# A decode kernel's tail: w4 in four pieces instead of five, and the first sums merged in two ways

## The chip, the cores and the metric

The kernel runs on one core of a Trainium2 chip. The metric is the device time of one execution in microseconds (us); less is better. Beside it stands the span, from the first to the last instruction of the program in the profile of the same kernel, which leaves out about 2 us at the edges. Each execution that was timed has one of each.

Engines are named as in the profile: PE is TensorE's matmuls, PEld its weight loads, DVE is VectorE, ACT is ScalarE. `L226` is a line of the kernel.

## The reference, cut to what matters

One token passes through two branches whose results are added to x: attention over a long cache with four key/value heads, and a small MLP.

```python
xn = _layernorm(x, axis=-1)
return x + _A_ref(xn, A_k_cache, A_v_cache, A_wq, A_wo) + _B_ref(xn, B_w1, B_w2, B_w3, B_w4)
# _A_ref: ... softmax(q k^T) v ... @ wo       caches of 4 x 65536 x 128 each
# _B_ref: ... h2 = gelu(layernorm(x1) @ w3) @ w4;  return x1 + h2     w4 is 3584 x 1024
```

About 170 MB are read and 2 KB written. The last thing read is w4: 28 rows of 128x1024 numbers in the kernel's layout (a "row" below is one of these 28, 256 KB of bfloat16).

## The kernel before

The loads stand in one queue and come in order (the pieces of w4 landed at 384.1, 391.4, 394.6, 395.8 and 396.4 us in the trace before); w4 is the last, in pieces of 8, 12, 5, 2 and 1 rows, so that its rows can be used while the next pieces come.

```python
W4_PIECES = (8, 12, 5, 2, 1)
FIRST = 3
AT_ONCE = 1
NARROW = 8
AHEAD = 5
...
for n in W4_PIECES:
    go(out=t[:, c0 * D:(c0 + n) * D], in_=w4_v[:, c0:c0 + n, :].rearrange("p c n -> p (c n)"))
```

The first 20 rows are "wide": two matmuls of 512 columns each into `psB`. The last 8 rows are "narrow": four matmuls of 256 columns into two other banks, `quarters`, so that four 32-column tiles of the array work side by side (in the trace before the first four start within 0.01 us, at 394.59 us, and take 0.28 us each). Between the fifth and the sixth narrow row the sums of the wide rows and of the attention are put into `quarters` by two small fp32 matmuls ("injection").

```python
early = sum(W4_PIECES[:AT_ONCE])
compute_w4(0, FIRST)
with tc.issue_after(tail["gathered"]):
    compute_w4(FIRST, early)
projected = project(HKV - 1)                       # attention, last head, into psB
with tc.issue_after(projected):
    compute_w4(early, FC - NARROW)                 # wide rows
sums = ogpool.tile([64, 512], F32, name="sums", tag="og")
nc.vector.tensor_tensor(out=sums[:], in0=psB[0:64, :], in1=tail["o"], op=ALU.add)
...
narrow_rows(FC - NARROW, FC - NARROW + AHEAD, start=True)
...
for h in range(2):                                 # fp32, 64x64 tiles
    nc.tensor.matmul(quarters[h][64 * h:64 * h + 64, 0:256], lhsT=pick[:]..., rhs=sums[:, 256 * h:256 * (h + 1)],
                     start=False, stop=False, tile_position=(0, 64 * h), skip_group_check=True)
narrow_rows(FC - NARROW + AHEAD, FC)
out_t = ogpool.tile([64, 2, 256], BF16, name="out_t", tag="og")
nc.scalar.copy(out=out_t[:, 0, :], in_=quarters[0][0:64, 0:256])
nc.vector.tensor_copy(out=out_t[:, 1, :], in_=quarters[1][64:128, 0:256])
nc.scalar.dma_start(out=out[0, 0, :].rearrange("(j n) -> j n", j=2), in_=out_t[31:33].rearrange("p h n -> p (h n)"))
```

## Time and profile before

| | before |
|---|---|
| median time, 3 runs | 401.07 us (400.98 to 402.7) |
| span of the profiled execution | 398.6 us |
| last landing of w4 | 396.44 us |
| end of the last matmul | 396.77 us |

From the page of the kernel before: the span, the engines' busy time, and the load queue with packets, MB and its share of the 16 DMA engines' time.

```profile
span 398.6 us, 2575 instructions
...
PE 225.4 (57%) x1360; PEld 44.0 (11%) x866; DVE 210.7 (53%) x160; ACT 27.1 (7%) x35; POOL 5.8 (1%) x29
...
q1 hardware_dynamic: 4128, 169.87, 98.9%
```

No compute engine is near full; the load queue is. The kernel is bound by its stream, and a change to its tail can hardly do more than shift what happens between the end of the stream and the end of the program. The chain that ended last in the kernel before (start, duration, what; its last four steps) says the same:

```profile
363.32 33.11 DMA big<-in_B_w_dram
396.44 0.04 issue
396.48 0.34 PE pm_r L501 x4
396.84 0.43 DVE out_t L522
```

The last landing, at once four matmuls, the cast, the store. TensorE in this stretch of the kernel before (start, duration, line, what, count, and in brackets the idle time before it and what ended that):

```profile
388.28 1.90 PE L227 MATMUL psB<-big,oT 128*32 128x512 bf16 x16
391.49 2.77 PE L227 MATMUL psB<-big,hT 128*32 128x512 bf16 x24 [1.30 <-DMA big<-in_B_w_dram]
394.59 0.73 PE L501 MATMUL pm_r<-big,hT 128*32 128x256 bf16 x20 [0.34 <-DMA big<-in_B_w_dram]
395.25 0.65 PE L516 MATMUL pm_r<-sums,pick 64*64 64x256 f32 x4
395.83 0.40 PE L501 MATMUL pm_r<-big,hT 128*32 128x256 bf16 x8
396.48 0.29 PE L501 MATMUL pm_r<-big,hT 128*32 128x256 bf16 x4 [0.24 <-DMA big<-in_B_w_dram]
```

The last four matmuls waited 0.24 us for the last row, so everything before them was done in time. And TensorE stood idle for 1.30 us before the 12-row piece.

### The profile page before, as it was taken

To read this page: it belongs to the slowest core of one execution; us is meant where nothing else is said; L and a number is where in the kernel's file an instruction comes from. 1 tells how busy PE (TensorE), PEld (TensorE's weight loads), DVE (VectorE), ACT (ScalarE), POOL (GpSimd) and SP (SyncE) were. 2 spreads that over 40 slices of the span, in tenths; PEclk is the share of its full clock that TensorE was granted. 3 is DMA by queue.
4 is the path that set the end of the run, shared out by engine and by line. 5 is a ranking of instruction groups with operands and counts; after the bars stand their busy time and mean duration, and the time that the engine had idled before them with its cause. 6 is when DMAs were issued, how large, how long until landed. Compare 5 with 4: busy or idle time off the path is not lost.

```text
span 398.6 us, 2575 instructions
## 1 busy us (share of the span) xinstructions
PE 225.4 (57%) x1360; PEld 44.0 (11%) x866; DVE 210.7 (53%) x160; ACT 27.1 (7%) x35; POOL 5.8 (1%) x29
## 2 busy tenths in 40 slices
PE   0251960591569238733974296519462955394986
PEld 0210000010100010011001010200020101010132
DVE  0610010974296559633963795269439942894141
ACT  1001020003000200020002000200110001002000
POOL 2000000000000000000000000000000000000000
PEclk9995996596869787966695889679956896698799
DMA  9998999999999999999999999999999998999996
GB/s 421 421 443 376 446 427 480 454 421 421 416 428 427 421 467 449 427 421 427 423 441 421 447 454 434 416 427 421 441 436 427 447 447 383 416 462 424 413 432 257
DMA packets 4144, 170.03 MB, mean 427 GB/s; under 512 B 419, under 2 KB 421, under 8 KB 678
## 3 DMA queue, kind: packets, MB, share of 16 engines
q1 hardware_dynamic: 4128, 169.87, 98.9%
q8 instruction: 9, 0.15, 0.2%
q14 instruction: 1, 0.01, 0.0%
q10 hardware_dynamic: 6, 0.00, 0.0%
HBM read 169.87 MB, written 0.00 MB: 426 GB/s over the span
## 4 chain that ended last, share of the span: by engine, by line
DMA 56%; DVE 21%; PE 17%; ACT 2%; another core or an unknown queue 2%; issue 1%; SPq 0%; DVEq 0%; ACTq 0%
DMA big<-in_A_k_cache_dram 42%; DVE big L360 15%; PE sc L365 11%; DMA big<-in_B_w_dram 8%; DMA big<-in_A_wq_dram 6%; PE oacc L415 4%; DVE p_sb L386 2%; DVE mx L370 2%; ACT p_sb L383 2%; PE psq L290 1%; SPq L187 0%; PE pm_mx L372 0%; DVE m L374 0%; PE pm_mx L379 0%
## 5 line engine op out<-in xcount | busy, mean ns | idle before, releaser
L365 PE MATMUL sc<-big,qdiag 128*128 128x512 bf16 x512 | 129.6, 414 | 66.5 <-DVE big L360 61.0
L360 DVE STREAM_TRANSPOSE big<-big 128x4096 f32<-128x4096 f32 x32 | 139.4, 4413 | 50.1 <-DMA big<-in_A_k_cache_dram 50.1
L415 PE MATMUL oacc<-big,p_sb 128*32 128x512 bf16 x512 | 43.2, 504 | 34.5 <-DVE p_sb L386 34.5
L370 DVE TENSOR_REDUCE mx<-sc 128x1 f32<-128x2048 f32 x8 | 18.3, 2292 | 29.9 <-PE sc L365 29.9
L365 PEld LDWEIGHTS <-qdiag 128*128 128x128 bf16 x128 | 13.2, 103 | 178.3 <-issue 145.7
L383 ACT ACTIVATE p_sb<-sc,nball 128x2048 bf16<-128x2048 f32 x8 | 15.7, 1968 | 220.8 <-DVE nball L381 220.8
L386 DVE STREAM_TRANSPOSE p_sb<-p_sb 128x2048 bf16<-128x2048 bf16 x8 | 18.5, 2311 | 18.0 <-ACT p_sb L383 18.0
L415 PEld LDWEIGHTS <-p_sb 128*32 128x32 bf16 x512 | 16.2, 122 | 58.2 <-DVE p_sb L386 35.1
L290 PE MATMUL psh<-big,ln_rep_b 128*32 128x512 bf16 (+1 forms) x64 | 12.4, 942 | 8.9 <-DMA big<-in_B_w_dram 8.9
L455 PE MATMUL o_acc<-big,oT 128*1 128x512 bf16 x48 | 13.2, 447 | 2.4 <-ACT p_sb L383 2.4
L372 PE MATMUL pm_mx<-ident_f,mx 128*1 128x128 f32 x8 | 2.4, 296 | 19.1 <-DVE mx L370 19.1
L424 DVE SCALAR_TENSOR_TENSOR og<-oacc,wb,og 128x512 f32<-128x512 f32 x4 | 3.0, 751 | 18.5 <-PE oacc L415 18.5
L329 DVE STREAM_TRANSPOSE h_row<-h_row 128x896 bf16<-128x896 bf16 x1 | 1.1, 1111 | 22.0 <-ACT h_row L328 22.0
L241 PE MATMUL pm_ln<-ln_rowsum_a,ones_f 128*128 128x1 f32 x2 | 0.6, 348 | 12.8 <-DVE ln_rowsum_a L239 12.8
L437 PE MATMUL pm_e<-ol,sel8big 128*128 128x129 f32 x8 | 2.3, 370 | 9.7 <-DVE ol L436 9.7
L314 POOL COPY qdiag<-qx 32x32 bf16<-32x32 bf16 x16 | 3.3, 204 | 278.7 <-PE sc L365 250.7
L290 PE MATMUL psq<-big,ln_rep_a 128*32 128x512 bf16 x64 | 5.0, 479 | 3.7 <-DMA big<-in_A_wq_dram 3.7
L232 DVE STREAM_TRANSPOSE x_t<-x_row 32x256 bf16<-32x256 bf16 x4 | 2.5, 615 | 8.4 <-DMA x_row<-in_A_x_dram 8.3
L466 DVE TENSOR_TENSOR big<-o_acc,big 1x512 f32<-1x512 f32 x2 | 1.4, 679 | 10.3 <-PE o_acc L455 10.3
L227 PE MATMUL psB<-big,hT 128*32 128x512 bf16 x40 | 4.8, 380 | 1.4 <-DMA big<-in_B_w_dram 1.3
L302 DVE CAST q_row<-psq 128x512 bf16<-128x512 f32 x1 | 0.7, 692 | 7.6 <-PE psq L290 7.6
L379 PE MATMUL pm_mx<-ident_f,rep 1*128 1x1 f32 x8 | 1.8, 229 | 5.0 <-DVE rep L376 5.0
(100 smaller groups left out, 71.9 us busy)
## 6 DMA issues: line engine op xcount, KB each, us to landing
big<-in_A_wo_dram SPq DMA_DIRECT2D x1, 8192.0 KB, 35.7
big<-in_B_w_dram SPq DMA_DIRECT2D x1, 7168.0 KB, 38.1
big<-in_B_w_dram SPq DMA_DIRECT2D x3, 2048.0 KB, 35.5
big<-in_B_w_dram SPq DMA_DIRECT2D x1, 3072.0 KB, 29.5
big<-in_B_w_dram SPq DMA_DIRECT2D x1, 1280.0 KB, 32.2
big<-in_B_w_dram SPq DMA_DIRECT2D x1, 512.0 KB
big<-in_B_w_dram SPq DMA_DIRECT2D x1, 256.0 KB, 33.1
big<-in_A_k_cache_dram SPq DMA_DIRECT2D x8, 42.2
```

The lines of the kernel that those rows point to most:

```text
L227: return nc.tensor.matmul(psB[32 * j:32 * j + 32, :], lhsT=lhsT.to_broadcast([lhsT.shape[0], 32]), rhs=rhs, start=start, stop=False, tile_ ...
L232: nc.vector.transpose(out=x_t[32 * a:32 * a + 32].rearrange("p c j -> p (c j)"), in_=x_row[:, 256 * a:256 * (a + 1)].rearrange("p (i c) -> ...
L290: nc.tensor.matmul(acc[32 * q:32 * q + 32, i, 0:n], lhsT=rep[:, c, :], rhs=cols(c, i, q), start=(c == 0), stop=(c == DC - 1), tile_positio ...
L314: nc.gpsimd.tensor_copy(out=qdiag[at, LEAD:].rearrange("p (x c) -> p x c", x=4)[:, :, 32 * a:32 * a + 8], in_=qx[at, :, 8 * g:8 * g + 8])
L360: nc.vector.transpose(out=words, in_=words)
L365: nc.tensor.matmul(sc[:, e, :], lhsT=qdiag[:, c0:c0 + P], rhs=cols[:, s, e, :, b2, :, r], start=(s == 0 and b2 == 0 and r == 0), stop=(s = ...
L370: nc.vector.reduce_max(out=mx[:], in_=sc[:].rearrange("p e n -> p (e n)"), axis=AX.X)
L383: nc.scalar.activation(out=p_sb[:], in_=sc[:], func=ACTF.Exp, bias=nball[:, b:b + 1], scale=SCALE, accum_out=group["lall"][:, b:b + 1])
L386: nc.vector.transpose(out=flat, in_=flat)
L415: mm = nc.tensor.matmul(oacc[32 * q:32 * (q + 1), :], lhsT=pT[:, e, 32 * t:32 * (t + 1)], rhs=vt[:, :, e, t, :], start=(e == 0 and t < 4), ...
L424: nc.vector.scalar_tensor_tensor(out=og[:], in0=oacc[:], scalar=wb[:, 1:2], in1=og[:], op0=ALU.mult, op1=ALU.add)
L455: nc.tensor.matmul(tail["rows"][0:1, h2, :], lhsT=oT[g][:, j:j + 1], rhs=wt[:, g, j, 512 * h2:512 * (h2 + 1)], start=(g == 0 and j == 0), ...
```

## The change

The intent: one load less in the tail (9, 13, 5, 1 rows), and the sums brought over more cheaply. The attention's part is injected early, in TensorE's idle time. The wide rows' sums are copied out as two halves, one by ScalarE and one by VectorE; the first is injected between the narrow rows, the second is added by VectorE in the cast that it does anyway. So one injection is left between the narrow rows where there were two.

```diff
-W4_PIECES = (8, 12, 5, 2, 1)
-FIRST = 3
-AT_ONCE = 1
-NARROW = 8
+W4_PIECES = (9, 13, 5, 1)
+FIRST = 6
+NARROW = 6
 AHEAD = 5
 ... (order of the first rows and of the gather: cut)
+    def inject(h, lhsT, rows, start):
+        return nc.tensor.matmul(quarters[h][64 * h:64 * h + 64, 0:256], lhsT=lhsT, rhs=rows, start=start,
+                                stop=False, tile_position=(0, 64 * h), skip_group_check=True).ins
+
     with tc.issue_after(projected):
+        for h in range(2):
+            begun = inject(h, pick[:].rearrange("p j r -> p (j r)"), tail["o"][0:64, 256 * h:256 * (h + 1)], True)
+    with tc.issue_after(begun):
         compute_w4(early, FC - NARROW)
-    sums = ogpool.tile([64, 512], F32, name="sums", tag="og")
-    nc.vector.tensor_tensor(out=sums[:], in0=psB[0:64, :], in1=tail["o"], op=ALU.add)
+    nc.scalar.copy(out=sums[0][:], in_=psB[0:64, 0:256])
+    nc.vector.tensor_copy(out=sums[1][:], in_=psB[0:64, 256:512])
 ...
-    narrow_rows(FC - NARROW, FC - NARROW + AHEAD, start=True)
-    for h in range(2):
-        nc.tensor.matmul(quarters[h]..., rhs=sums[:, 256 * h:256 * (h + 1)], ...)
+    narrow_rows(FC - NARROW, FC - NARROW + AHEAD)
+    inject(0, ident_f[0:64, 0:64], sums[0][:], False)
     narrow_rows(FC - NARROW + AHEAD, FC)
 ...
-    nc.vector.tensor_copy(out=out_t[:, 1, :], in_=quarters[1][64:128, 0:256])
+    nc.vector.tensor_tensor(out=out_t[:, 1, :], in0=quarters[1][64:128, 0:256], in1=sums[1][:], op=ALU.add)
```

## The prediction

> **What bounds the kernel.** The load stream. The page gives the DMA queue 98.9% of the 16 engines' time, 170 MB at 427 GB/s, over a span of 398.6 us. The chain that ended last finishes with w4's last piece, its four 128x256 matmuls, the output cast and the store. Up to the w4 stage the change leaves every engine's instructions as they were, so only the last 20 us count.
>
> **The w4 landings before**, from the semaphore records (last of 16 increments): 384.13 (8 rows), 391.44 (12), 394.55 (5), 395.79 (2), 396.44 us (1). The pieces cost 7.32, 3.11, 1.24 and 0.64 us. A fit to the 12-row and 1-row pieces gives 0.607 us a row plus 0.036 us a piece. So one piece fewer saves about 0.04 us and no more. Estimated landings after: 384.7, 392.7, 395.73 (5 rows), 396.37 (1 row).
>
> **What moves on TensorE** (durations from the timeline). Before, between the landings of the 5-row piece and of the last row: 20 narrow matmuls issue in 0.46 us (394.59 to 395.05). The fp32 injection of the sums starts 0.20 us later, at 395.25, though the sums were done at 394.97. The next narrow matmul starts at 395.83: last narrow matmul to next narrow matmul, 0.78 us. Eight more follow, and PE then waits 0.24 us for the last landing (396.48 start, 396.77 end). The chain is thus DMA-bound with 0.24 us to spare, because 1.88 us lie between those landings.
>
> After, only 0.64 us lie between them, while PE must do 20 narrow matmuls, an injection and 4 more. The injection is halved in work, but not, I think, in time: the two 64-column tiles ran side by side (their passes start at 395.252/395.259 and 395.519/395.526), so one alone has the same two passes in sequence. [...] I expect 0.78 us again.
>
> Sum: 395.73 + 0.04 + 0.46 + 0.78 + 0.29 = 397.30 us for the last matmul's end, against 396.77: **+0.53 us on the critical path**, now bound by PE instead of by the last landing.
>
> **Off the path.** The tail projection's injection (before: part of the sums' addition, 0.68 us on DVE) moves into PE's idle time before the 13-row piece. Those 26 wide matmuls, 0.104 us apart, issue by 395.3 us, before the 5-row piece lands. ScalarE's copy of 64x256 (0.37 us by the output cast) ends near 396.1, the injection can start at 396.43: no wait. VectorE's second copy ends near 396.6. The final cast plus add should cost the same as the cast (0.43 us; 684 ns for the 512-column add, scaled, gives about 0.42).
>
> **Prediction.** 401.07 + 0.5 = 401.6 us; 8 in 10: 400.9 to 402.5 us. Faster by over 2% 0.005, within 2% 0.985, slower by over 2% 0.01.
>
> **Right or wrong in the profile.** Four w4 pieces, last landing 0.0 to 0.1 us earlier; no DMA wait before the last four matmuls, since PE gets to them late; about 0.78 us between narrow matmuls around the one injection; last matmul end near 397.3; output stage of unchanged length.
>
> **What would make it wrong.** A single injection of one column tile taking about half the 0.78 us: then the change is nearly neutral. PE's idle stretch before the 13-row piece grows from 1.3 to about 1.8 us; if the clock drops (it stood at 1.0 through the stage), the wide rows take twice as long: +2 us. Run-to-run noise (400.98 to 402.7) is larger than the effect.

## The result, and the profile after

| | before | after |
|---|---|---|
| median time, 6 runs each | 401.05 us (400.88 to 402.70) | 402.51 us (401.19 to 402.78) |
| span of the profiled execution | 398.6 us | 400.8 us |
| spans of the six runs after | | 399.2, 399.2, 399.3, 399.3, 400.7, 400.8 us |

The ratio after to before is 1.0022 (95% interval 0.9998 to 1.0045); the medians would give 1.0036. Every ratio here is the mean time of one kernel's runs over that of the other's of the same rounds, so it is not quite the ratio of the medians. The verdict is "same" at 2%, and the direction (longer) is as predicted. But the median, 402.51 us, lies a hundredth above the upper end of the predicted range (402.5 us), and the spans fall into two groups. The point forecast, 401.6 us, lies between the groups and near none of the six times. The median is a poor guide here besides: two of its four long times (402.32 and 402.78 us) have short spans (399.2 and 399.3 us) and a further microsecond outside the span, which is not explained below. So there was something to find out.

The profiled execution after belongs to the long group. Its chain that ended last (last five steps) no longer ends with a load:

```profile
392.93 4.30 PE psB L226 x23
397.23 0.91 PE pm_r L522 x10
398.15 0.57 PE pm_r L505 x2
398.72 0.28 PE pm_r L522 x4
399.02 0.43 DVE out_t L532
```

TensorE in the same execution of the changed kernel:

```profile
387.87 1.90 PE L226 MATMUL psB<-big,oT 128*32 128x512 bf16 x16 [0.32 <-DVE oT L448]
389.71 0.65 PE L505 MATMUL pm_r<-big,pick 64*64 64x256 f32 x4
392.93 3.68 PE L226 MATMUL psB<-big,hT 128*32 128x512 bf16 x22 [2.58 <-DMA big<-in_B_w_dram]
...
396.84 1.31 PE L522 MATMUL pm_r<-big,hT 128*32 128x256 bf16 x16
398.08 0.64 PE L505 MATMUL pm_r<-sums_a,ident_f 64*64 64x256 f32 x2
398.65 0.29 PE L522 MATMUL pm_r<-big,hT 128*32 128x256 bf16 x4
```

The idle stretch before the 13-row piece is 2.58 us here, and that piece's wide matmuls run until 397.5 us, past the last landing (396.61 us). The clock tells why. The clock granted to TensorE changes only at the edges of a fixed grid of 3.41 us in these traces (all 72 steps from one change to the next, in before and after together, are whole multiples of it); the next two fences show stretches of that grid: the stretch, its length, then each engine's busy time with the number of instructions, the granted clock (PEclk, 1.00 is full), and the DMA's share and GB/s. Before:

```profile
389.98:393.39 3.41, 2.11 (x20) 1.01 (x19) 0.00 (x0) 0.00 (x0) 0.00 (x0) 1.00 0.95 397
393.39:396.80 3.41, 2.80 (x44) 1.18 (x40) 0.68 (x1) 0.00 (x0) 0.00 (x0) 1.00 0.49 195
```

After:

```profile
390.79:394.20 3.41, 1.27 (x12) 0.67 (x13) 0.00 (x0) 0.00 (x0) 0.00 (x0) 1.00 0.92 384
394.20:397.61 3.41, 3.41 (x30) 1.64 (x28) 0.00 (x0) 0.11 (x1) 0.00 (x0) 0.50 0.24 96
```

Before, TensorE was busy 2.11 us (62%) of the stretch with its idle time, and kept its clock. After, it was busy only 1.27 us (37%), and the next stretch, with the wide rows in it, ran at half clock: the wide matmuls, 0.104 us apart at full clock, stand 0.21 us apart.

To see how firm this is I counted every such stretch that ends between 30 and 396 us in ten traces (before, after and the first eight experiments). Of 619 stretches at full clock, 174 were followed by half clock and 445 were not. All 445 had TensorE busy for at least 0.425 of the time (by the profile's durations, in which the ends of matmuls are modelled); of the 174, 173 had at most 0.41 (one, in e_one, had 0.47). In before and after alone it is 125 stretches: the 35 followed by half clock had 0.374 at most, the 90 others 0.426 at least. In the other direction, the clock came back after stretches with at least 0.77, and never with 0.76 or less. The three later traces keep the first bound; the second is less firm, for in e_noinj the clock came back once after a share of 0.69. So in these traces the clock follows the busy share of one 3.41 us stretch. It did not take a stretch without any work: the one with 1.27 us of work and 2.14 us of idle time in it, in the trace after, was enough.

### The profile page after: what moved, and what is told of

Read it like the earlier page. It is cut to its first block, busy times and chain, and to the rows that moved or that the text cites. A ratio compares the mean times of both kernels' runs of the same rounds, so it can differ in the third digit from the quotient of the medians.

```text
span 400.8 us, 2573 instructions
## 1 busy us (share of the span) xinstructions
PE 230.1 (57%) x1358; PEld 45.9 (11%) x864; DVE 210.5 (53%) x160; ACT 27.4 (7%) x36; POOL 5.8 (1%) x29
## 4 chain that ended last, share of the span: by engine, by line
DMA 55%; DVE 21%; PE 19%; another core or an unknown queue 2%; ACT 2%; issue 1%; SPq 0%; DVEq 0%; ACTq 0%
DMA big<-in_A_k_cache_dram 42%; DVE big L359 15%; PE sc L364 11%; DMA big<-in_B_w_dram 8%; DMA big<-in_A_wq_dram 5%; PE oacc L414 4%; DVE p_sb L385 2%; DVE mx L369 2%; ACT p_sb L382 2%; PE psq L289 1%; PE psB L226 1%; PE pm_r L522 0%; DVE m L373 0%; PE pm_mx L371 0%
## 5 line engine op out<-in xcount | busy, mean ns | idle before, releaser
L414 PE MATMUL oacc<-big,p_sb 128*32 128x512 bf16 x512 | 44.8, 527 | 34.5 <-DVE p_sb L385 34.5
L414 PEld LDWEIGHTS <-p_sb 128*32 128x32 bf16 x512 | 17.1, 127 | 59.6 <-DVE p_sb L385 35.1
L457 PE MATMUL o_acc<-big,oT 128*1 128x512 bf16 x48 | 11.9, 413 | 2.4 <-ACT p_sb L382 2.4
L226 PE MATMUL psB<-big,hT 128*32 128x512 bf16 x44 | 6.8, 464 | 4.4 <-DMA big<-in_B_w_dram 4.4
```

Of the source, the lines that this page charges most:

```text
L226: return nc.tensor.matmul(psB[32 * j:32 * j + 32, :], lhsT=lhsT.to_broadcast([lhsT.shape[0], 32]), rhs=rhs, start=start, stop=False, tile_ ...
L414: mm = nc.tensor.matmul(oacc[32 * q:32 * (q + 1), :], lhsT=pT[:, e, 32 * t:32 * (t + 1)], rhs=vt[:, :, e, t, :], start=(e == 0 and t < 4), ...
L457: nc.tensor.matmul(tail["rows"][0:1, h2, :], lhsT=oT[g][:, j:j + 1], rhs=wt[:, g, j, 512 * h2:512 * (h2 + 1)], start=(g == 0 and j == 0), ...
```

## The experiments

Eleven kernels were run, each run five rounds against the kernel before on the same chip. The 95% intervals of three ratios lie wholly above 1 (r_after, e_pieces, e_one). Differences of some tenths of a microsecond are read from the spans. Two theories were set against each other for the long group. "Clock": the longer idle stretch lets a 3.41 us window fall under about 40% busy, and the wide rows then run at half clock. "Stream": the last landing of w4 comes later in the long runs. For the short group, which is still some 0.5 us above before, the theory was that the one injection stands on TensorE's path because only 0.64 us are left between the last two landings; the rival was that the new handling of the sums costs time by itself.

### The changed kernel again (r_after)

No edit.

> The changed kernel again, for the distribution. Theory (clock): the stretch in which TensorE waits for the 13-row piece is 1.8 to 2.6 us long; where a 3.41 us clock window holds more than about 2.05 us of it, the clock is halved for the next window and the wide rows run late. So two groups of times, near 401.3 and near 402.7 us (about half of the runs each), spans near 399.2 and 400.8. Rival (stream): the slow runs come from a later last landing of w4; then a slow profile shows the landing about 1.5 us later at full clock.

Six times: 401.11, 401.68, 402.39, 402.53, 402.71, 403.15 us; spans 399.1, 399.1, 400.4, 400.4, 400.5, 400.7. The ratio is 1.0032 (1.0019 to 1.0046). The two groups are there again. The profiled execution was a long one (400.4 us): busy 39% in its window from 389.01 us (2.07 us of it idle), half clock from 392.42 us (columns as above):

```profile
389.01:392.42 3.41, 1.34 (x12) 0.43 (x9) 0.00 (x0) 0.00 (x0) 0.00 (x0) 1.00 0.93 398
392.42:395.83 3.41, 3.11 (x16) 1.33 (x17) 0.00 (x0) 0.00 (x0) 0.00 (x0) 0.50 0.71 290
```

Its last landing came at 396.41 us, no later than before's 396.44, so "stream" has nothing to stand on (it asked for a landing about 1.5 us later at full clock; the other long trace, after, has 396.61). With the first result, 6 of 12 executions are long. Two of the six have a trace, both at half clock; for the other four it is inferred from their spans.

Of the kernel before, 33 executions ran: 29 have spans of 398.6 to 399.1 us, and 4 have 399.8 to 400.0. So the kernel before has a few long ones too; none of them has a trace, and what makes them long is not shown.

### Keeping TensorE busy in the gap (e_fill)

```diff
+    warm = ps_O.tile([P, 512], F32, name="warm", tag="oacc")
+    def keep_warm(n):                      # result unused
+        wt = st.tiles["w4"]
+        for _ in range(n):
+            mm = nc.tensor.matmul(warm[0:32, :], lhsT=hT[:, 0:1].to_broadcast([P, 32]), rhs=wt[:, 0:512], start=True,
+                                  stop=True, tile_position=(0, 0), skip_group_check=True)
+        return mm.ins
     with tc.issue_after(begun):
+        warmed = keep_warm(6)
+    with tc.issue_after(warmed):
         compute_w4(early, FC - NARROW)
```

> The changed kernel with six extra 512-column matmuls (1.28 us, result unused) in TensorE's idle stretch before the 13-row piece. Theory (clock): no run is slow any more; all near 401.2 to 401.5 us, span 399.2, granted clock 1.0 from about 373 us to the end, the wide rows of the 13-row piece 0.104 us apart. Rival (stream or noise): the slow group stays as frequent as in the changed kernel. Left over in every run is the injection on the path: 0.3 to 0.5 us above the kernel before.

Five times from 401.08 to 401.38 us, spans 399.1 to 399.4, ratio 1.0007 (0.9995 to 1.0019): the long group is gone. (Five executions alone would be few against 6 of 12; e_noinj below, with the same pieces and the same filler, has no long one among six either.) The clock window of e_fill that holds the rest of the gap (columns as above) has TensorE busy for 2.34 us and full clock:

```profile
390.98:394.39 3.41, 2.34 (x21) 1.03 (x20) 0.00 (x0) 0.00 (x0) 0.00 (x0) 1.00 0.92 385
```

TensorE's timeline of e_fill, from the filler (`warm`) on; the six took 1.47 us from the first start to the last end, where 1.28 was expected:

```profile
390.10 1.47 PE L517 MATMUL warm<-big,hT 128*32 128x512 bf16 x6
392.63 2.98 PE L226 MATMUL psB<-big,hT 128*32 128x512 bf16 x26 [1.07 <-DMA big<-in_B_w_dram]
395.71 0.73 PE L534 MATMUL pm_r<-big,hT 128*32 128x256 bf16 x20
396.37 0.64 PE L505 MATMUL pm_r<-sums_a,ident_f 64*64 64x256 f32 x2
396.94 0.29 PE L534 MATMUL pm_r<-big,hT 128*32 128x256 bf16 x4
```

More work on TensorE took the long group away, and what changed with it in the trace is the clock. This is also the first sight of the changed tail at full clock: the last matmul ends at 397.23 us (the prediction said 397.30), and no bracket stands before the last four matmuls: they do not wait for the last landing (396.32 us).

### The injection taken out (e_noinj)

Half of this output is wrong on purpose: it lacks the wide rows' sums. (The comparison with the reference still let it pass; its tolerance is wider than that part.)

```diff
-    inject(0, ident_f[0:64, 0:64], sums[0][:], False)
```

(on top of e_fill)

> The changed kernel with the filler, and without the one injection between the narrow rows; half of the output is wrong on purpose. Theory (the injection alone holds up the end): the last four matmuls now wait for the last landing, near 396.3 us; last matmul end near 396.65 against 397.23 with the filler and the injection; span 398.5 to 398.6 us against 399.1, about 0.5 to 0.6 us. Rival (the 20 narrow matmuls or the last landing hold it up): a gain under 0.2 us.

Spans 398.6 to 398.9 us, median 398.75, against 399.2 with the injection (e_fill): 0.45 us shorter. (They were run at other times. The kernel before had the same median span, 398.7 us, in both.) The times are 400.56 to 400.89 us. In the profiled execution the whole stream was a third of a microsecond later (last landing 396.65 us), so absolute times are not compared; what counts is that all 24 narrow matmuls now stand in one group that ends 0.33 us after the last landing, with the last four starting 0.04 us after it (396.69 us), as TensorE's timeline of e_noinj shows:

```profile
392.98 2.98 PE L226 MATMUL psB<-big,hT 128*32 128x512 bf16 x26 [0.80 <-DMA big<-in_B_w_dram]
396.05 0.93 PE L534 MATMUL pm_r<-big,hT 128*32 128x256 bf16 x24
```

So the injection was the thing in the way. It is little work, but it costs 0.78 us from narrow matmul to narrow matmul (397.87 to 398.65 us in the trace after, 396.17 to 396.94 in e_fill; 0.78 with two injections before). Half of the injections cost all of the time.

### Each half of the change alone (e_pieces, e_sums)

e_pieces is the kernel before with only the new pieces:

```diff
-W4_PIECES = (8, 12, 5, 2, 1)
+W4_PIECES = (9, 13, 5, 1)
-NARROW = 8
+NARROW = 6
```

> The kernel before with the pieces 9, 13, 5, 1 and six narrow rows alone; the sums are still added by VectorE and both halves injected. Theory (the pieces cost, not the sums): fast runs at or above the changed kernel's fast runs, 401.3 to 401.6 us, PE-bound at the end with 0.78 us around the injections; slow runs at least as frequent, as the idle stretch is longer by the missing early injections. Rival (the new handling of the sums costs): as the kernel before, 401.05 us.

e_sums is the changed kernel with only the pieces put back:

```diff
-W4_PIECES = (9, 13, 5, 1)
+W4_PIECES = (8, 12, 5, 2, 1)
-NARROW = 6
+NARROW = 8
```

> The changed kernel with the old pieces 8, 12, 5, 2, 1 and eight narrow rows: the new handling of the sums alone. Theory: the last four matmuls wait for the last landing again (about 0.2 us), so the time is that of the kernel before within 0.1 us in fast runs, and slow runs are rare, as the idle stretch before the 12-row piece is about 0.7 to 1.4 us. Rival (sums cost): 401.3 us or more.

The pieces carry all of the loss. e_pieces: spans 399.1, 399.3 and four of 400.7 to 400.9, ratio 1.0043 (1.0030 to 1.0056). Its profiled execution, a short one, ends its last matmul at 397.23 us, like e_fill. Its idle stretch was the longest, 3.39 us, split by chance over two windows with 47% and 53% busy, and so it kept the clock:

```profile
392.60 2.98 PE L227 MATMUL psB<-big,hT 128*32 128x512 bf16 x26 [3.39 <-DMA big<-in_B_w_dram]
```

e_sums: spans 398.6 to 399.0, ratio 0.9994 (0.9982 to 1.0006), and the wait of 0.24 us before the last four matmuls is back:

```profile
396.53 0.29 PE L522 MATMUL pm_r<-big,hT 128*32 128x256 bf16 x4 [0.24 <-DMA big<-in_B_w_dram]
```

The new handling of the sums costs nothing that these runs can tell. It is no gain in span either, since the old handling was hidden under the stream already.

### More room before the last landing (e_two)

```diff
-W4_PIECES = (9, 13, 5, 1)
+W4_PIECES = (9, 12, 5, 2)
-NARROW = 6
+NARROW = 7
```

> The changed kernel with pieces 9, 12, 5, 2 and seven narrow rows: 1.24 us instead of 0.64 us between the last two landings. Theory (the injection is on the path only because the last piece follows too soon): TensorE is through 20 narrow matmuls and the injection (1.28 us) just as the last piece lands, then does 8 matmuls; last matmul end near 396.8 against 397.23 in the changed kernel's full-clock runs, span 398.7 to 398.9 us in fast runs. The idle stretch before the 12-row piece is 0.6 us shorter, so slow runs are rarer, under a third. Rival (the changed handling costs 0.4 us wherever the pieces end): span 399.1 us.

With 1.23 us between the last two landings, TensorE comes out even with the stream, in its timeline of e_two:

```profile
392.21 2.77 PE L226 MATMUL psB<-big,hT 128*32 128x512 bf16 x24 [1.47 <-DMA big<-in_B_w_dram]
395.30 0.73 PE L522 MATMUL pm_r<-big,hT 128*32 128x256 bf16 x20 [0.33 <-DMA big<-in_B_w_dram]
395.96 0.64 PE L505 MATMUL pm_r<-sums_a,ident_f 64*64 64x256 f32 x2
396.53 0.40 PE L522 MATMUL pm_r<-big,hT 128*32 128x256 bf16 x8
```

The last eight matmuls start 0.04 us after the landing at 396.49 us and end at 396.93 (0.1 us later than I had said). Short spans are 398.8 to 398.9 us, as expected: same number of loads, same handling of the sums, and the 0.4 us are gone. My guess for the long group missed: three of six (399.9 to 400.1 us) and not under a third. The profiled execution was a short one, so no trace shows a long one of this kernel. The stretch that its trace shows, 1.47 us, would by itself leave a window over half busy, so why half of its executions are long stays open.

### The filler in the kernel before (b_fill), and in the better half of the change (e_sums_fill)

b_fill is the kernel before with the six extra matmuls after `projected`:

```diff
     with tc.issue_after(projected):
+        warmed = keep_warm(6)
+    with tc.issue_after(warmed):
         compute_w4(early, FC - NARROW)
```

> The kernel before with the six extra matmuls in its idle stretch, as a control of the filler's own cost. Theory: the filler costs nothing and the kernel before has no slow runs to remove, so the span stays at 398.6 to 398.9 us and the time at 400.9 us, same within 0.1 us. Rival (the extra matmuls or their reads slow the stream or delay the 12-row piece's rows): 0.2 us or more above the kernel before.

All six spans are 398.7 us, times 400.84 to 400.96, ratio 0.9991 (0.9978 to 1.0004). The filler costs nothing that can be measured here. My expectation that the kernel before had no long runs to remove was wrong: in this lot it had two, at 399.8 us.

e_sums_fill is e_sums with the same filler:

```diff
     with tc.issue_after(begun):
+        warmed = keep_warm(6)
+    with tc.issue_after(warmed):
         compute_w4(early, FC - NARROW)
```

> The new handling of the sums with the old pieces 8, 12, 5, 2, 1 and the filler: the version that should be best. Theory: always the full clock and bound by the last landing; all spans 398.6 to 398.8 us, times 400.6 to 400.8 us, none above 401.2. Rival: runs a microsecond longer still appear, as in the kernel before (two spans of 399.8 us among eleven).

Spans 398.7 to 399.0, times 400.70 to 401.07 us, ratio 0.9987 (0.9969 to 1.0005), none above 401.2. Two spans (399.0) were above the 398.8 that I had set as the limit. Part of the filler ran interleaved with the wide rows and pushed them back, but the last four matmuls still waited 0.24 us for the last landing. Both versions are steady, and each of their 12 executions (400.70 to 401.07 us) is shorter than every one of the changed kernel's 12 (401.11 and up). They were run at other times. Against the kernel before the intervals still include 1: the two versions are equal to it within what was measured, apart from its rare long spans, of which they show 0 in 12 against 4 in 33, too few to be sure of.

### A single accumulator (e_one, e_one_idle, e_one_short)

If all rows are narrow and go to one bank, there is nothing to merge at all:

```diff
-    mm = nc.tensor.matmul(psB[32 * j:32 * j + 32, :], lhsT=..., rhs=rhs, ..., tile_position=(0, 32 * j))
+    for h in range(2):
+        q = 2 * j + h
+        mm = nc.tensor.matmul(psB[32 * q:32 * q + 32, 0:256], lhsT=..., rhs=rhs[:, 256 * h:256 * (h + 1)], ...,
+                              tile_position=(0, 32 * q))
 ... (copies, injection, second cast: gone; ten filler matmuls)
+    nc.scalar.copy(out=out_t[:], in_=psB[:, 0:256])
+    nc.scalar.dma_start(out=out[0, 0, :].rearrange("(q n) -> q n", q=4), in_=out_t[0:P:32, :])
```

> A version meant to beat both: all of w4, the last projection and w2 accumulate as four 256-column parts in one PSUM bank, so there are no sums to copy or inject at the end; one ScalarE cast and a store of four 512-byte rows; pieces 9, 13, 5, 1; ten filler matmuls keep the clock. Theory: bound by the last landing again (near 396.3 us), last matmul end near 396.65, cast 0.37 us, store issued near 397.1 instead of 397.4: span 398.3 to 398.5 us, time near 400.6 us, no slow runs. Rival (stores of four rows land later, or the narrow rows cost elsewhere): 398.7 us or more.

A clear miss: spans 400.3 to 400.8 us, ratio 1.0034. The 5-row piece landed at 397.14 us in its trace, over a microsecond late; the timeline of e_one from there (TensorE, ScalarE and the issue of the store):

```profile
393.73 1.79 PE L228 MATMUL psB<-big,hT 128*32 128x256 bf16 x46
397.18 0.93 PE L228 MATMUL psB<-big,hT 128*32 128x256 bf16 x24 [1.66 <-DMA big<-in_B_w_dram]
398.15 0.37 ACT L528 CAST out_t<-psB 128x256 bf16<-128x256 f32 x1 [30.48 <-PE psB L228]
398.56 0.61 ACTq L529 DMA_DIRECT2D out_dram<-out_t  x1
```

The landing of a piece is 16 semaphore increments in the trace, called shares here. For the 5-row piece fifteen had come by 395.97 us; the sixteenth came at 397.14, 1.17 us later. Before that, one packet of the instruction queue had run: 16 KB, 1.02 us, from 393.16 us. (In the trace before, that queue's last two packets, 16 KB each, started at 383.79 and 397.84 us, the last one after the stream.) The queues of this kernel between 393.0 and 394.3 us (packets, MB, share of the 16 engines' time):

```profile
q1 hardware_dynamic: 102, 0.45, 87.6%
q8 instruction: 1, 0.02, 4.9%
```

The theory: four matmuls a row instead of two, and the filler, had moved a fetch of instructions to before the end of the stream, and it held up the late share by running on the same DMA engine. This link was not shown: the trace shows neither whose instructions the packet held nor which DMA engine moved it. The version without the filler (the edit is against e_one):

```diff
-    with tc.issue_after(begun):
-        begun = keep_warm(10)
     with tc.issue_after(begun):
         compute_w4(early, FC)
```

> The same without the filler: TensorE idles 3 us or more before the 13-row piece, so the clock drops in most runs. Theory: at half clock the narrow rows of the 5-row piece take about 1 us and the last four matmuls 0.4 us, so most runs are 0.3 to 0.6 us longer than with the filler (less than the 1.4 us of the changed kernel, since a narrow row takes half the time of a wide one); a few are equal. Rival (the clock does not matter without the wide rows): equal in all runs.

Here the packet started at 396.02 us and no share was late. Spans are 399.0, 399.1, and four of 399.4 to 399.6; the profiled one (399.1) ran at half clock from 392.52 us and finished 0.33 us after the last landing all the same. So a half clock, which lasted to 395.94 us, cost this layout little there; the four longer executions have no trace, and were not pursued. (In the trace before, at full clock, the narrow rows start 0.11 us apart and the wide ones 0.22 us.) The forecast (0.3 to 0.6 us longer than with the filler) missed, because the version with the filler had the trouble of its own. To test the fetch theory, 28 early matmuls were taken out (w2 is multiplied by a zero vector in this kernel, and one of its eight rows is enough to open the accumulator; the edit is against e_one):

```diff
-        for c in range(DC):
+        for c in range(1):
             for j in range(2):
                 row_acc(j, g_col[:], wt[:, 1, c, 512 * j:512 * (j + 1)], start=(c == 0))
```

> The single-accumulator version with the filler, and with 28 matmuls fewer early on (w2 is multiplied by a zero vector; one of eight rows stays, so the result is unchanged). In the longer version a fetch of 16 KB of instructions ran on one DMA engine for 1.0 us at 393.16 us[...]. Theory (instruction fetch): with fewer instructions before it, the fetch moves behind the last rows, the 5-row piece lands near 395.7 to 395.9 us again, and the span falls from 400.3 to 400.8 to 398.8 to 399.1 us. Rival (the narrow layout or the filler disturbs the stream itself): landing near 397 and span above 400 us as before.

The packet moved to 395.68 us, and no share was late (of the last row, fifteen shares had landed by 396.35 us and the sixteenth at 396.39), the 5-row piece landed at 395.76 us, and the spans fell to 399.0 to 399.3 us (I had said 398.8 to 399.1). What the fetch theory forecast came: a later packet, and the piece on time, in one trace. How a packet makes a share late is not shown. "The layout or the filler disturbs the stream" falls, for both are still there. What is left above the kernel before is the store, in the timeline of e_one_short:

```profile
395.80 0.93 PE L228 MATMUL psB<-big,hT 128*32 128x256 bf16 x24 [1.48 <-DMA big<-in_B_w_dram]
396.77 0.37 ACT L528 CAST out_t<-psB 128x256 bf16<-128x256 f32 x1 [28.89 <-PE psB L228]
397.18 0.60 ACTq L529 DMA_DIRECT2D out_dram<-out_t  x1
```

It is issued 0.17 us earlier than before (397.18 against 397.35 us), but its issue takes 0.60 us for four rows of 512 bytes, where before it took 0.27 us for two rows of 1 KB. From there to the end of the span it is 1.8 us instead of 1.26. This version beats neither of the others.

## Why the prediction was right, and where it was not

- **The stream bounds the kernel; one piece less saves at most 0.04 us.** Nothing contradicts it, and nothing shows it. Last landings in single traces lie between 396.28 and 396.65 us whatever the pieces (e_one with its late share apart), a scatter that hides 0.04 us.
- **One injection costs as much as two, and stands on the path.** Right. The last matmul was put at 397.30 us; at full clock it ended at 397.23 us (e_fill, e_pieces). Taking the injection out gave 0.45 us of span. In the trace before, the 0.78 us between the starts of two narrow matmuls are 0.20 us to the first fp32 pass on 64x64 tiles, 0.27 to the second and 0.31 to the next narrow matmul (395.05, 395.25, 395.52, 395.83 us); in e_sums_fill it was 0.81. How much of that is the change of tiles and how much the fp32 passes, no run separates.
- **The handling of the sums is off the path, and cast plus add costs what the cast did.** Right: 0.43 us each, and e_sums runs like the kernel before.
- **"PE's idle stretch before the 13-row piece grows from 1.3 to about 1.8 us; if the clock drops ... +2 us."** This is the step that failed. The mechanism was named, but as a remote chance, and the stretch was put too short.

  The stretch measured 2.58 us in the trace after and 2.38 in its repeat. The work before it ended at 390.35 us in both, about 0.6 us earlier than the forecast implies, and in the trace after the piece also landed 0.2 us later (392.89 us against 392.7). One reason lies further back, which the prediction did not look at: the clock's grid has another phase in each of these traces (edges at 389.98 us in before, 390.79 in after, 389.01 in r_after, 390.98 in e_fill), and the later the clock comes back before the last attention work, the later this work ends. Over the thirteen traces, it came back between 370.2 and 373.5 us, and TensorE finished the attention between 382.9 and 384.5 us, in nearly the same order. The trace before was a late one (372.91 and 384.08 us), after and its repeat were earlier (370.31 and 383.06; 371.94 and 383.64). In e_two and e_noinj, late ones too, the work before the stretch (or the filler) ended at 390.74 and 390.78 us and not at 390.35. So the 1.3 us of one trace was no fixed size.

  And I had not used what the trace before already held in its windows: those followed by half clock were at most 0.32 busy, the others at least 0.44, so a window with 2 us of idle time was near the limit that the ten traces then put between 0.41 and 0.425. With 2.4 to 2.6 us idle it depends on the phase of the window whether the share falls below that. By an estimate from these figures (a window has to hold 2.0 us of the stretch, and every phase is equally likely) it should in 52 to 58% of the executions. The long group is 6 of 12, about 1.4 us longer each.
- **The time.** 401.6 us was meant for the short group, at 398.6 + 0.5 us of span. The direction is no luck, for the injection's 0.5 us stands in the short group. That the six times average 0.9 us above the kernel before, not far from the forecast 0.5, is luck: the average mixes two groups and some long times outside the span. The short group's spans are 0.5 us longer (399.1 to 399.3 against 398.6 to 398.9), but its usual times are 401.1 to 401.3, some 0.25 us above before's 401.0. The difference lies outside the span: where the kernel keeps the old sums (before, b_fill, e_pieces) time minus span is mostly 2.2 us, with the new sums (after, e_fill, e_sums, e_two) mostly 2.0. No run tells what that 0.2 us is. Single executions with a further microsecond in the time and not in the span occur with both, and are not explained either.

## What to carry to other kernels

When the last piece of a stream lands, what matters is not how much work is left but how much time lies between the last landings for the work that must come in between: keep the small merging steps (here 0.78 us, for one injection as for two) before the last landing by at least their own length. On TensorE, look at the busy share of each clock window before a stretch that is on the critical path; if waiting for data brings it under some 40%, as it did in the two long traces here (37% and 39%), a few matmuls with no use are a cheap thing to try (they took the long group away here, and gained nothing in a kernel that rarely had one). Look at more than one execution before you take an idle time as given. And compare spreads, not only medians: two groups of times can hide a mechanism that has not been found yet.
